# Attention and two gated layers on one core: the second layer's periods dealt in another order

## The chip, the cores and the metric

The kernel runs on one core of a Trainium2 chip. The metric is the device time of one execution in microseconds (us). TensorE (PE in the profile) does the matmuls, VectorE (DVE) and ScalarE (ACT) the work on their results, GpSimd (POOL) some sums and the DMAs that add into memory, SyncE (SP) issues the other DMAs.

## What is computed

A channel attention makes x (6016 tokens by 256), a first gated layer (silu) follows, and a second one (sigmoid), each with 1536 hidden units:

```python
def _moe2_ref(x, w_gate, w_val, w_out):
    gate = 1.0 / (1.0 + np.exp(-(x @ w_gate)))
    val = x @ w_val
    return (gate * val @ w_out).astype(np.float32)
```

## The kernel before

Every product of two fp32 matrices is made of three passes (`mm3`, lines 106 to 109): each operand is split into a rounded high part (a cast on ScalarE) and a low part (a subtraction on VectorE), and high·high, high·low and low·high are summed in PSUM. So a "product" below is three matmuls with 128 rows and 512 columns (448 in one of the six pairs of token blocks), and a "split" is a cast `hh` (line 618) and a subtraction `hl` (line 626).

The tokens are worked in six pairs of blocks, the hidden units in 12 blocks of 128. One step, a pair and a block of hidden units, is a **period**. The second layer has 72 of them, numbered here n = 0 to 71; the first twelve belong to the first pair, and so on. A period computes gate and value of two token blocks with seven products instead of eight (Strassen's scheme in Winograd's form), named after the operand: B11, T1, T4, T2, B21, T3, B22. T4 belongs to the period before. Four banks of PSUM hold them:

- Z ("g"): B11, then T2 added, then T3 added. After B11 ScalarE copies it to A, after T2 it copies it out as `g1`, after T3 two engines read it: ScalarE copies it to D (line 792), VectorE adds `e5` to it, which gives `v1` (line 798). Two engines never read one bank at once: the second waits for the first. B11 of the next period overwrites Z.
- B ("g"): T1, copied to `e5`; then B22 is added, and VectorE adds it to `g1` (line 804).
- A ("v"): B21 is added, ScalarE makes the gate `sg0` of it (line 785).
- D ("v"): T4 is added a period later, VectorE multiplies it by the gate (`fourth`, lines 551 and 553).

The sigmoid of `g1` (line 733) and the other gated product follow early in the next period. The gated values (`hs`) of six periods make a **team**, whose product with `w_out` is again Strassen's: seven kinds of operand, three blocks each, so 21 **output products**. They are done in the six periods that follow, three or four in each, between the seven others (`out`, `out_product`). Each needs its operand split first (`split_high`, `split_low`); `split_high(ahead)` goes at most so many splits ahead of the products. `hidden` lends the buffers of split values, three each for `hh` and `hl`. Results of output products are gathered in `r` (`gather`, called by `flush`): for the first team of a pair mostly by copies on ScalarE, for the second by additions on VectorE. `third_sum` and `first_sum` add gated values; some additions go as accumulating DMAs from POOL's queue (`more`, line 571).

Nothing reorders the work: each engine runs its instructions in the order in which the program's lines issue them (`manual_schedule`). In each period, hooks (`at("early")`, `at("ACT")`, `at("DVE")`, `at("end")`) also run the splits of the next pair's seven input operands (`pair_high` at periods 3 to 9 of every twelve, `pair_low` at 4 to 10, lines 366 and 369) and the sums that three or four of these need, as additions on POOL (`pair_sums`, `pair_sum`, line 398). "Position" below is n modulo 12; at positions 0 and 6 a team starts.

Of the kernel before, what the change touches and what calls it, by code (L numbers as in the profile page):

```python
# [10 lines left out]
F32 = mybir.dt.float32  # L11
# [6 lines left out]
P = 128  # L18
# [7 lines left out]
def kernel(  # L26
# [411 lines left out]
    def hidden(name):  # L438
        return ip3.tile([P, 512], F32R, tag=name, name=name)
# [171 lines left out]
    def split_high(ahead):  # L611
        while job and job["split"] < min(LAST, job["done"] + ahead):
# [77 lines left out]
    def period(it, pv, n, outs=()):  # L690


        s = {}
        slot = slots.popleft() if slots else {}
        outs = deque(partial(out_mm, *o, c) for o in outs for c in range(KC))
        n1 = n - len(stream0)
# [5 lines left out]
        def fourth(s):  # L702
            l, p, f = s["it"]
            w = hw[p]
            product(s["v0"], s["it"], T4, A22, False)
            gated(s["h"][:, 0, :w] if l else s["v0"], s["v0"], s["sg0"], l and f % 2)

        def split(ahead):
            if n1 >= 0:
                split_high(ahead)  # L710
                split_low()

        def out(count):
            for _ in range(count):
                if outs:
                    outs.popleft()()
                elif n1 >= 0:
                    out_product()

        if it:  # L720
            l, p, f = it
            w = hw[p]
            s["it"] = it
            act = (AF.Silu, AF.Sigmoid)[l]
# [5 lines left out]
        if pv:  # L730
            pl, pp, pf = pv["it"]
            pw = hw[pp]
            nc.scalar.activation(out=pv["g1"], in_=pv["g1"], func=(AF.Silu, AF.Sigmoid)[pl])  # L733
            gated(pv["v1"], pv["v1"], pv["g1"], pl and pf % 2 == 0)
        flush()
        if n1 > 0 and n1 % HALF == 0:
            team_start(n1 // HALF - 1)
        if n1 > 0 and pf % 2:
            third_sum(n1 - 1)
        split(2)  # L740
        if not it:
            while job["done"] < LAST:
                split(3)
                out_product()
                flush()
            return
        nc.scalar.copy(A, Z)  # L747
        if pv and pl == 0:
            hh1, hl1 = hidden("hh"), hidden("hl")
            nc.scalar.copy(hh1[:, :pw], pv["v1"])  # L750
            nc.vector.tensor_sub(hl1[:, :pw], pv["v1"], f32(hh1[:, :pw]))  # L751
            hid[pl, pp, 1, pf] = hh1, hl1
            fourth(pv)
        e5 = sp.tile([P, 512], F32, tag="e5", name="e5")[:, :w]
        if pv and pl:
            nc.scalar.copy(e5, B)
            if n1 > 0:
                split_high(3)
            fourth(pv)
            gw_load(n1 + 2)  # L760
            split_low()
            if pf % 2 == 0:
                first_sum(n1 - 1)
        at("early")
        if not (pv and pl):
            nc.scalar.copy(e5, B)
        else:
            out(1 if n1 % 2 == 0 else 0)
# [4 lines left out]
        if pv and pl == 0:  # L773
            hh0, hl0 = hidden("hh"), hidden("hl")
            nc.scalar.copy(hh0[:, :pw], pv["v0"])
            nc.vector.tensor_sub(hl0[:, :pw], pv["v0"], f32(hh0[:, :pw]))
            hid[pl, pp, 0, pf] = hh0, hl0
        flush()
        if n1 % 2 == 0:
            split(3)  # L780
        if n1 >= 0:
            out(2 if outs else 1)
            at("DVE")
        s["sg0"] = ip2.tile([P, 512], F32, tag="sg", name="sg")[:, :w]
        nc.scalar.activation(out=s["sg0"], in_=A, func=act)  # L785
        if n1 < 0:
            out(2)
            at("ACT")
            at("DVE")
        product(Z, it, T3, S3, False)  # L790
        D = s["v0"] = gv_bank("v")[:, :w]
        nc.scalar.copy(D, Z)  # L792
        if l:
            s["h"] = h_tile()
            s["v1"] = s["h"][:, 1, :w]
        else:
# [352 lines left out]
```

## Time and profile before

| | |
|---|---|
| median of 3 runs | 1227.27 us (1225.7 to 1228.14) |
| the profiled execution, its own time | 1227.86 us |
| its span, first to last instruction | 1225.8 us |
| TensorE busy | 96% of the span |
| VectorE, ScalarE busy | 74%, 69% |
| second layer's periods 1 to 71 | from 684 to 1202 us |
| the last team's products, after the last period | 1202 to 1226 us |

A matmul's end is modelled in the profile, so that busy time of TensorE hides gaps; the gap is seen in the start times, which are 0.227 us apart for 512 columns when nothing waits. The granted clock of TensorE is full in the second layer.

### The profile page before, as it was taken

To read this page: it belongs to the slowest core of one execution; us is meant where nothing else is said; L and a number is where in the kernel's file an instruction comes from. 1 tells how busy PE (TensorE), PEld (TensorE's weight loads), DVE (VectorE), ACT (ScalarE), POOL (GpSimd) and SP (SyncE) were. 2 spreads that over 40 slices of the span, in tenths; PEclk is the share of its full clock that TensorE was granted. 3 is DMA by queue.
4 is the path that set the end of the run, shared out by engine and by line. 5 is a ranking of instruction groups with operands and counts; after the bars stand their busy time and mean duration, and the time that the engine had idled before them with its cause. 6 is when DMAs were issued, how large, how long until landed. Compare 5 with 4: busy or idle time off the path is not lost.

```text
span 1225.8 us, 15986 instructions
## 1 busy us (share of the span) xinstructions
PE 1178.7 (96%) x5290; PEld 966.1 (79%) x5290; DVE 911.7 (74%) x1382; ACT 847.5 (69%) x1591; POOL 281.1 (23%) x327
## 2 busy tenths in 40 slices
PE   8898999999999999999999999999999999999997
PEld 7787777788899788888888677777777777778895
DVE  6798888876566566666665577887887888887877
ACT  6665667765566676677666677677777777777775
POOL 0043655553200200200200111311311311311121
PEclk9899999999999999999999999999999999999999
DMA  9662434766301301201430578988988988988995
GB/s 334 245 221 87 131 107 158 260 224 207 111 1 28 97 26 35 95 26 35 155 99 1 168 200 248 263 247 244 267 251 239 275 246 239 277 239 248 271 251 140
DMA packets 100946, 214.43 MB, mean 175 GB/s; under 512 B 10240, under 2 KB 35840, under 8 KB 100864
## 3 DMA queue, kind: packets, MB, share of 16 engines
q1 hardware_dynamic: 86896, 188.65, 46.2%
q0 software_dynamic: 13824, 24.65, 11.1%
q8 instruction: 41, 0.67, 0.2%
q14 instruction: 41, 0.34, 0.1%
q10 hardware_dynamic: 144, 0.13, 0.0%
HBM read 150.87 MB, written 37.88 MB: 154 GB/s over the span
## 4 chain that ended last, share of the span: by engine, by line
PE 62%; DVE 11%; ACT 4%; issue 4%; DMA 1%; POOL 0%; SPq 0%; DVEq 0%; ACTq 0%; POOLq 0%
PE g L107 10%; PE g L108 9%; PE g L109 9%; PE v L107 4%; PE v L108 4%; PE y L108 4%; PE v L109 4%; PE y L109 4%; PE y L107 4%; PE at L108 3%; PE at L109 3%; PE at L107 3%; DVE hl L626 2%; DVE g L804 2%; ACT v L792 1%
## 5 line engine op out<-in xcount | busy, mean ns | idle before, releaser
L571 POOL DMA_DIRECT2D hs<-hs x96 | 83.6, 914 | 466.1 <-DVE hl L626 197.3
L626 DVE TENSOR_TENSOR hl<-hs,hh 128x512 fp32r<-128x512 f32 (+1 forms) x216 | 152.5, 714 | 20.5 <-ACT hh L618 19.7
L733 ACT ACTIVATE g<-g 128x512 f32<-128x512 f32 (+1 forms) x120 | 74.7, 623 | 121.9 <-DVE g L804 121.9
L618 ACT CAST hh<-hs 128x512 fp32r<-128x512 f32 (+1 forms) x216 | 130.1, 609 | 4.6 <-PE y L109 1.4
L792 ACT COPY v<-g 128x512 f32<-128x512 f32 (+1 forms) x120 | 67.2, 560 | 65.8 <-PE g L109 65.1
L772 ACT COPY g<-g 128x512 f32<-128x512 f32 (+1 forms) x120 | 69.4, 578 | 44.7 <-PE g L109 44.0
L798 DVE TENSOR_TENSOR hs<-g,e 128x512 f32<-128x512 f32 (+1 forms) x72 | 48.9, 680 | 50.1 <-ACT v L792 50.1
L804 DVE TENSOR_TENSOR g<-g,g 128x512 f32<-128x512 f32 (+1 forms) x120 | 79.7, 664 | 0.0
L107 PE MATMUL g<-xh,gw 128*128 128x512 f32 x180 | 73.0, 405 | 5.7 <-DVE hs L798 4.9
L785 ACT ACTIVATE sg<-v 128x512 f32<-128x512 f32 (+1 forms) x120 | 71.1, 592 | 3.7
L107 PE MATMUL g<-qh,wh 128*128 128x512 f32 x168 | 66.8, 397 | 6.6 <-ACT wh L187 5.3
L798 DVE TENSOR_TENSOR v<-g,e 128x512 f32<-128x512 f32 (+1 forms) x48 | 32.4, 675 | 53.9 <-ACT v L792 53.9
L747 ACT COPY v<-g 128x512 f32<-128x512 f32 (+1 forms) x120 | 68.0, 567 | 4.8 <-PE g L109 0.3
L108 PE MATMUL g<-xl,gw 128*128 128x512 f32 x180 | 70.3, 391 | 0.0
L109 PE MATMUL g<-xh,gw 128*128 128x512 f32 x180 | 70.2, 390 | 0.0
L109 PE MATMUL g<-qh,wl 128*128 128x512 f32 x168 | 66.3, 395 | 1.9 <-DVE wl L196 1.9
L108 PE MATMUL g<-ql,wh 128*128 128x512 f32 x168 | 66.0, 393 | 0.0
L108 PE MATMUL y<-hl,ow 128*128 128x512 f32 (+1 forms) x144 | 57.2, 397 | 9.1 <-DVE hl L626 9.0
L451 ACT CAST hh<-v 128x512 fp32r<-128x512 f32 x48 | 28.1, 585 | 48.5 <-DVE v L449 48.5
L107 PE MATMUL v<-qh,wh 128*128 128x512 f32 x144 | 57.9, 402 | 3.3 <-DVE hl L457 3.3
L751 DVE TENSOR_TENSOR hl<-v,hh 128x512 fp32r<-128x512 f32 (+1 forms) x48 | 32.7, 681 | 32.4 <-ACT hh L750 32.4
L109 PE MATMUL v<-qh,wl 128*128 128x512 f32 x144 | 56.6, 393 | 0.0
(230 smaller groups left out, 3650.2 us busy)
## 6 DMA issues: line engine op xcount, KB each, us to landing
gw<-gd SPq DMA_DIRECT2D x144, 448.0 KB, 5.5
ow<-od SPq DMA_DIRECT2D x84, 384.0 KB, 5.1
hs<-hs POOLq DMA_DIRECT2D x80, 256.0 KB, 6.7
wraw<-in_w_dram SPq DMA_DIRECT2D x24, 768.0 KB, 5.4
vraw<-in_v_t_dram SPq DMA_DIRECT2D x11, 512.0 KB, 3.8
gd<-w2h SPq DMA_DIRECT2D x12, 448.0 KB, 2.6
gd<-w2l SPq DMA_DIRECT2D x12, 448.0 KB, 3.5
yd<-yo SPq DMA_DIRECT2D x20, 256.0 KB, 2.9
```

The costliest lines, as they stand in the source:

```text
L107: nc.tensor.matmul(ps, sh, mh, start=start, stop=False, skip_group_check=more)
L108: nc.tensor.matmul(ps, sh, ml, start=False, stop=False, skip_group_check=more)
L109: nc.tensor.matmul(ps, sl, mh, start=False, stop=stop, skip_group_check=more)
L571: nc.gpsimd.dma_start(out=to, in_=t, accum_op=ALU.add)
L618: nc.scalar.copy(h, src)
L626: nc.vector.tensor_sub(lo, src, f32(h))
L733: nc.scalar.activation(out=pv["g1"], in_=pv["g1"], func=(AF.Silu, AF.Sigmoid)[pl])
L772: nc.scalar.copy(s["g1"], Z)
L785: nc.scalar.activation(out=s["sg0"], in_=A, func=act)
L792: nc.scalar.copy(D, Z)
L798: nc.vector.tensor_add(s["v1"], Z, e5)
L804: nc.vector.tensor_add(s["g1"], s["g1"], B)
```

## The change

`period` is divided into two functions: `period` for the first layer, where the order of the instructions stays, and `team_period` for the second layer. In the second layer:

- `hidden` lends four buffers each for `hh` and `hl` (for the whole kernel), and `split_high` may be four ahead of the output products; its argument is now the most splits that one call makes.
- After T3, VectorE adds `v1` first, and ScalarE copies Z to D second.
- The copies of Z to A and of B to `e5` come before any split of the period; two splits follow, whose `hl` stand behind `fourth`; one more `hh` and `hl` stands behind the copy to `g1`, one behind the gate, two more at the end where a buffer is free.
- No output product stands between T4 and T2. There is one after B21, and at the period's end three in even and two in odd periods (before: one more after T4 in even periods, two at the end).
- `third_sum` stands ahead of the gathering.

```diff
     def hidden(name):
-        return ip3.tile([P, 512], F32R, tag=name, name=name)
+        return ip3.tile([P, 512], F32R, tag=name, name=name, bufs=4)
...
-    def split_high(ahead):
-        while job and job["split"] < min(LAST, job["done"] + ahead):
+    def split_high(most):
+        while job and most and job["split"] < min(LAST, job["done"] + 4):
+            most -= 1
...
+    def team_period(it, pv, n, outs):
...
+        if n and pf % 2:
+            third_sum(n - 1)
         flush()
...
         nc.scalar.copy(A, Z)
...
+        nc.scalar.copy(e5, B)
+        split_high(2)
+        fourth(pv)
+        split_low()
...
         product(Z, it, T2, S2, False)
         product(A, it, B21, A12, False)
...
+        split(1)
+        out(2 if outs else 1)
...
+        nc.scalar.activation(out=s["sg0"], in_=A, func=AF.Sigmoid)
+        at("DVE")
         flush()
+        split(1)
         product(Z, it, T3, S3, False)
         D = s["v0"] = gv_bank("v")[:, :w]
+        s["h"] = h_tile()
+        s["v1"] = s["h"][:, 1, :w]
+        nc.vector.tensor_add(s["v1"], Z, e5)
         nc.scalar.copy(D, Z)
+        at("ACT")
         product(B, it, B22, S4, False)
         nc.vector.tensor_add(s["g1"], s["g1"], B)
+        split(2)
...
-            out(max(2, len(outs)))
+            out(max(3 - n % 2, len(outs)))
```

VectorE's order in period 33 (position 9) before, from its addition to `g1` at the end of period 32 to its own `v1` (L626 is `hl`, L551 the product with the second gate, L553 `fourth`, L559 `first_sum`, L369 a split of the next pair's input, L798 `v1`):

```order
L804 TENSOR_TENSOR g_8825<-g_8825,g 128x512
L626 TENSOR_TENSOR hl<-hs,hh 128x512
L551 SCALAR_TENSOR_TENSOR hs<-hs,g_8825 128x512
L626 TENSOR_TENSOR hl<-hs,hh 128x512
L553 TENSOR_TENSOR hs<-v,sg 128x512
L626 TENSOR_TENSOR hl<-hs,hh 128x512
L559 TENSOR_TENSOR t<-hs 128x512
L369 TENSOR_TENSOR ql<-xs,qh 128x512
L798 TENSOR_TENSOR hs<-g,e_8879 128x512
```

and now (L627 is `hl`, L831 `v1`):

```order
L835 TENSOR_TENSOR g_8827<-g_8827,g 128x512
L551 SCALAR_TENSOR_TENSOR hs<-hs,g_8827 128x512
L553 TENSOR_TENSOR hs<-v,sg 128x512
L627 TENSOR_TENSOR hl<-hs,hh 128x512 x2
L559 TENSOR_TENSOR t<-hs 128x512
L627 TENSOR_TENSOR hl<-hs,hh 128x512
L369 TENSOR_TENSOR ql<-xs,qh 128x512
L627 TENSOR_TENSOR hl<-hs,hh 128x512
L831 TENSOR_TENSOR hs<-g,e_8875 128x512
```

Between `fourth` and `v1` stand six instructions now, three before; ahead of `fourth` stand fewer.

ScalarE's order at the end of the same period and the start of the next, with the engines that each instruction waits for, before (L785 is the gate, L792 the copy to D, L668 a gathering, L618 `hh`, L733 the sigmoid of `g1`):

```order
L785 ACTIVATE sg<-v 128x512 [waits PE_49]
L792 COPY v<-g 128x512 [waits DVE_49,PE_49]
L668 COPY r<-y 128x512
L618 CAST hh<-hs 128x512 [waits Activation_49]
L366 CAST qh<-ql 128x512
L733 ACTIVATE g_8901<-g_8901 128x512 [waits DVE_49]
```

and now (L832 is the copy to D, L788 the sigmoid, L801 the copy to A):

```order
L669 COPY r<-y 128x512 [waits PE_49]
L619 CAST hh<-hs 128x512 [waits DMASW5_49,Activation_49]
L832 COPY v<-g 128x512 [waits DVE_49]
L366 CAST qh<-ql 128x512
L788 ACTIVATE g_8901<-g_8901 128x512 [waits DVE_49]
L801 COPY v<-g 128x512 [waits PE_49,Activation_49]
```

The copy to D waits for VectorE, whose `v1` waits for TensorE; a split and the gathering moved ahead of it.

TensorE's order where a team starts (period 30, position 6), from T4 (`v`) to the team's first output product (`y`), before:

```order
L107 MATMUL v<-xh,gw 128x512
L108 MATMUL v<-xl,gw 128x512
L109 MATMUL v<-xh,gw 128x512
L107 MATMUL y<-hh,ow 128x512
L108 MATMUL y<-hl,ow 128x512
L109 MATMUL y<-hh,ow 128x512
```

and now:

```order
L107 MATMUL v<-xh,gw 128x512
L108 MATMUL v<-xl,gw 128x512
L109 MATMUL v<-xh,gw 128x512
L107 MATMUL g<-xh,gw 128x512
L108 MATMUL g<-xl,gw 128x512
L109 MATMUL g<-xh,gw 128x512
L107 MATMUL v<-xh,gw 128x512
L108 MATMUL v<-xl,gw 128x512
L109 MATMUL v<-xh,gw 128x512
L107 MATMUL y<-hh,ow 128x512
L108 MATMUL y<-hl,ow 128x512
L109 MATMUL y<-hh,ow 128x512
```

The first output product stands two products later in its period.

## Rows read from the trace of the kernel before

**Rows 1.** Page, part 1: busy us (share of the span) and instructions by engine

```profile
PE 1178.7 (96%) x5290; PEld 966.1 (79%) x5290; DVE 911.7 (74%) x1382; ACT 847.5 (69%) x1591; POOL 281.1 (23%) x327
```

**Rows 2.** Windows by stage: us, busy time (instructions) by engine, clock, DMA share, GB/s

```profile
684.15:714.38 30.23, 26.77 (x105) 18.86 (x105) 17.70 (x26) 19.31 (x35) 7.08 (x6) 1.00 0.79 239
714.38:1120.26 405.88, 395.40 (x1701) 316.28 (x1700) 337.65 (x516) 304.06 (x566) 85.88 (x88) 1.00 0.87 250
```

**Rows 3.** Waits of TensorE's weight loads, 684 to 1202 us: total us, times, longest

```profile
PEld y L108 <- DVE hl L626: 11.7, 11, 1.3
PEld g L107 <- DVE hs L798: 10.6, 9, 1.4
PEld g L107 <- ACT v L747: 7.6, 17, 0.5
```

**Rows 4.** Timeline, ScalarE: the same sigmoid in periods 24 and 36 (start, duration, what)

```profile
857.36 0.63 ACT L733 ACTIVATE g<-g 128x512 f32<-128x512 f32 x1 [0.81 <-DVE g L804]
...
947.88 0.64 ACT L733 ACTIVATE g<-g 128x512 f32<-128x512 f32 x1 [0.81 <-DVE g L804]
```

**Rows 5.** Timeline, TensorE, period 33: first of B11, last of T4, last of T3, next B11

```profile
918.16 0.39 PE L107 MATMUL g<-xh,gw 128*128 128x512 f32 x1
...
919.97 0.39 PE L109 MATMUL v<-xh,gw 128*128 128x512 f32 x1
...
922.69 0.39 PE L109 MATMUL g<-xh,gw 128*128 128x512 f32 x1
...
924.96 0.39 PE L107 MATMUL g<-xh,gw 128*128 128x512 f32 x1
```

**Rows 6.** Timeline, VectorE, period 33: `fourth` and what follows, to `v1`

```profile
920.40 0.69 DVE L553 TENSOR_TENSOR hs<-v,sg 128x512 f32<-128x512 f32 x1 [0.20 <-PE v L109]
921.01 0.68 DVE L626 TENSOR_TENSOR hl<-hs,hh 128x512 fp32r<-128x512 f32 x1
...
922.21 0.68 DVE L369 TENSOR_TENSOR ql<-xs,qh 128x512 fp32r<-128x512 f32 x1
923.72 0.69 DVE L798 TENSOR_TENSOR hs<-g,e 128x512 f32<-128x512 f32 x1 [0.83 <-ACT v L792]
```

**Rows 7.** Timeline, ScalarE, period 33: the copy to D, and a cast behind it

```profile
923.12 0.57 ACT L792 COPY v<-g 128x512 f32<-128x512 f32 x1 [0.76 <-PE g L109]
...
924.60 0.63 ACT L366 CAST qh<-ql 128x512 fp32r<-128x512 f32 x1
```

**Rows 8.** Timeline, TensorE, period 30: a team's first output product waits for its `hl`

```profile
896.88 0.39 PE L107 MATMUL y<-hh,ow 128*128 128x512 f32 x1
898.13 0.50 PE L108 MATMUL y<-hl,ow 128*128 128x512 f32 x1 [0.86 <-DVE hl L626]
898.47 0.40 PE L109 MATMUL y<-hh,ow 128*128 128x512 f32 x1
```

**Rows 9.** Timeline, period 27 (position 3): VectorE and POOL, and the B11 behind it

```profile
873.51 2.34 DVE L626 TENSOR_TENSOR hl<-hs,hh 128x512 fp32r<-128x512 f32 x1
875.77 0.68 DVE L553 TENSOR_TENSOR hs<-v,sg 128x512 f32<-128x512 f32 x1
...
879.18 0.68 DVE L798 TENSOR_TENSOR hs<-g,e 128x512 f32<-128x512 f32 x1
...
873.66 1.63 POOL L398 TENSOR_TENSOR xs<-zl,ql 128x512 f32<-128x512 f32 x1
...
879.91 0.50 PE L107 MATMUL g<-xh,gw 128*128 128x512 f32 x1 [0.93 <-DVE hs L798]
```

**Rows 10.** Timeline, POOL, period 28 (position 4): the sum for T4 of the next pair

```profile
886.83 1.29 POOL L398 TENSOR_TENSOR xs<-ql,xs 128x512 f32<-128x512 f32 x1 [3.22 <-ACT v L792]
```

**Rows 11.** Timeline, TensorE, period 2, without output products: B11 waits for `v1`

```profile
689.55 0.50 PE L107 MATMUL g<-xh,gw 128*128 128x512 f32 x1 [0.69 <-DVE hs L798]
```

**Rows 12.** Timeline, VectorE, after the last period: splits 11 to 13, the last split, the last gathering

```profile
1213.30 1.70 DVE L626 TENSOR_TENSOR hl<-hs,hh 128x448 fp32r<-128x448 f32 x3
...
1220.97 0.61 DVE L626 TENSOR_TENSOR hl<-hs,hh 128x448 fp32r<-128x448 f32 x1
1222.34 0.62 DVE L680 TENSOR_TENSOR r<-r,at 128x448 f32<-128x448 f32 x1 [0.76 <-PE at L109]
```

More of the change, by code (lines that the diff above doesn't have):

```diff
@@ L700, in at @@
                 fn()
[L702 to L711, printed above, removed]
+        l, p, f = it
+        w = hw[p]
+        Z = gv_bank("g")[:, :w]
+        product(Z, it, B11, A11, True)
+        A = gv_bank("v")[:, :w]
+        B = gv_bank("g")[:, :w]
+        product(B, it, T1, S1, True)
+        if pv:
+            nc.scalar.activation(out=pv["g1"], in_=pv["g1"], func=AF.Silu)
+            nc.vector.tensor_mul(pv["v1"], pv["v1"], pv["g1"])
+        nc.scalar.copy(A, Z)
+        if pv:
+            parts(pv, 1, pv["v1"])
+            fourth(pv)
+        at("early")
+        e5 = sp.tile([P, 512], F32, tag="e5", name="e5")[:, :w]
+        nc.scalar.copy(e5, B)
+        product(Z, it, T2, S2, False)
+        product(A, it, B21, A12, False)
+        s["g1"] = sp2.tile([P, 512], F32, tag="g1", name="g1")[:, :w]
+        nc.scalar.copy(s["g1"], Z)
+        if pv:
+            parts(pv, 0, pv["v0"])
+        s["sg0"] = ip2.tile([P, 512], F32, tag="sg", name="sg")[:, :w]
+        nc.scalar.activation(out=s["sg0"], in_=A, func=AF.Silu)
+        for _ in range(2):
+            outs.popleft()()
+        at("ACT")
+        at("DVE")
+        product(Z, it, T3, S3, False)
+        D = s["v0"] = gv_bank("v")[:, :w]
+        nc.scalar.copy(D, Z)
+        s["v1"] = sp.tile([P, 512], F32, tag="t0", name="v1")[:, :w]
+        nc.vector.tensor_add(s["v1"], Z, e5)
+        product(B, it, B22, S4, False)
+        nc.vector.tensor_add(s["g1"], s["g1"], B)
+        while outs:
+            outs.popleft()()
+        at("end")
+        return s
+    def team_period(it, pv, n, outs):
+        s = {"it": it}
+        slot = slots.popleft() if slots else {}
+        outs = deque(partial(out_mm, *o, c) for o in outs for c in range(KC))
+        def at(point):
+            for fn in slot.get(point, ()):
+                fn()
         def out(count):
@@ L716, in out, with split @@
                     outs.popleft()()
-                elif n1 >= 0:
+                else:
                     out_product()
+        def split(most):
+            split_high(most)
+            split_low()
         if it:
```

102 lines of the change are left out of this document (39 added, 63 removed).

## The prediction, made before the changed kernel ran

> **What bounds the kernel now.** The page's first part [rows 1] says TensorE, busy 96% of the span, ahead of VectorE with 74%. The windows by stage come next [rows 2]: the change touches the second layer alone, so 684 us to the end, and the steady part of it, from the first team at 714 us, is where its new order acts. How much TensorE loses there is read from start times. One product takes 0.68 us (T4's last matmul ends the third product: 919.97 + 0.23 - 918.16 = 2.04) [rows 5]. Twelve periods hold 12 x 7 + 2 x 21 = 126 products, 85.7 us; the same sigmoid twelve periods apart is 90.5 us apart [rows 4]. So 4.8 us in twelve periods are waits, of which I can put 4.55 to places; the rest is spread over the starts and stays. The waits of the weight loads name them [rows 3]: a team's first output product waits for its `hl`, 11 times; B11 waits for `v1`, 9 times; T2 or another product of Z waits for a copy on ScalarE, 17 times. I made the list by position in the twelve: 1.14 us at position 6 [rows 8], 0.67 at 0, the same wait; 2.1 at positions 3 and 4, where POOL holds VectorE up [rows 9]; 0.32 each at 7 and 11, T2 behind the copy to A.
>
> **What the change takes away.** At a team's start the first output product stands two products (1.36 us) later, and its split stands behind fewer things: 1.14 and 0.67 go at a start where VectorE is in time. The copy to A stands ahead of splits and directly behind the sigmoid, so the two 0.32 go. The wait at position 3 is VectorE's lateness, to be worked out anew. No instruction is added or removed on any engine; SP's and POOL's DMAs keep their order, only their place in the period shifts by less than one period, and the landing that matters (accumulated `hs`, used some two periods on, 14 us) stays far off. In periods 1 to 5, which have no output products, B11 waits for both readers of Z in turn [rows 11]; 0.69 then 0.57 us is as long as 0.57 then 0.69, so nothing changes there. The first layer keeps its order; a fourth buffer there has no wait to remove.
>
> **What it adds: the copy to D now waits for VectorE, and B11 for the copy.** Take the quiet period 33, clock zero at B11's first matmul (918.16). T4's result can be read at 2.24, where `fourth` began; VectorE's instructions follow each other by 0.60 ((922.21 - 920.40) / 3) [rows 6]. T3's result can be read at 4.96, when the copy to D began [rows 7]. Before, VectorE had three instructions between `fourth` and `v1` and was free at 4.65; it sat idle 0.83 us until the copy was done [rows 6]. B11 is due at 6.80 after ten products (odd periods) [rows 5], at 7.48 after eleven (even). From the start of `v1` Z comes free after 0.69 + 0.03 + 0.57 + 0.06 = 1.35 us: its own duration, the copy's [rows 6, 7], and two handovers (923.12 + 0.57 to 923.72; 879.18 + 0.68 to 879.91) [rows 7, 9].
>
> With k instructions between `fourth` and `v1`, `v1` starts at 2.24 + 0.605 (k + 1), and Z is free 1.35 later: k = 3 at 6.3 (T3 decides), 4 at 6.6, 5 at 7.2, 6 at 7.8. Counted in the new order, k by position 0 to 11 is 4, 5, 3, 6, 5, 4, 5, 6, 4, 6, 5, 3 (before 2 to 4 everywhere). Even periods have 7.48 and are in time with all of them. Odd ones are not: k = 5 costs 0.43 (position 1), k = 6 costs 1.03 (positions 3, 7, 9). Each stall also costs 0.11 for the matmul that resumes (898.13 to 898.47 is 0.34 against 0.23) [rows 8]. First order: 0.43 + 3 x 1.03 + 4 x 0.11 = 4.0 us in twelve periods, against 4.55 taken away. By this alone the change would be worth nothing, and the second order decides.
>
> **Second order.** Each is a delay on an engine that no longer has slack.
> - Position 3: three sums on POOL, 1.63 us each. A VectorE instruction with both operands in SBUF waits until such a sum ends (873.66 + 1.63 = 875.29, the `hl` ends 0.56 later, having taken 2.34 us); one that reads PSUM does not (875.77, 0.68 us) [rows 9]. In the new order POOL comes to these sums at the end of position 2, from about 0.8 us before to 4.3 us after B11, and the first `hl` behind `fourth` (2.85) waits for the third: +1.3. Bounds: 0, were the sums over in time, and 3.2, were three instructions blocked as in period 27 (the first by 2.34 - 0.69 = 1.65, the two others together by about as much). I take 1.3, since POOL runs as soon as its queue lets it.
> - Position 4: the sum for the next T4, 1.29 us [rows 10], starts when the cast's low part is done (4.75) and holds one `hl` up: `v1` at 6.6, Z at 7.95, +0.45 and 0.11. Below: 0.
> - Position 5: the copy to D ends as B11 starts, a cast of the next pair stands behind it (0.52 from one start to the next, 924.60 to the next sigmoid) [rows 7], so the sigmoid starts at 0.36, and two gatherings stand ahead of `fourth`: +0.42 and 0.11. Below: 0.15.
> - Position 6: the same lateness, then `third_sum` and a gathering; the team's first `hl` ends at 4.1 and is wanted at 3.63: 0.56 and 0.22. So half of the team-start wait stays where the sixth period is full; at position 0 it goes.
> - Position 7: two casts behind the late copy, then a gathering before the copy to A; `hl` waits for `hh`: +0.37.
>
> Together 1.3 + 0.56 + 0.53 + 0.78 + 0.37 = 3.5, so 7.5 against 4.55: **+2.95 in twelve periods**, four times (periods 12 to 59) +11.8. Periods 6 to 11 have positions 6, 7, 9: 2.9 against 1.7, +1.2. Periods 60 to 71 have no next pair and 448 columns: by the same steps (product 0.595, VectorE 0.54 apart, (1.70 - 0.62) / 2 [rows 12]) 3.0 against 2.6, +0.4.
>
> **The end.** After the last period VectorE is the longest queue. The fourth buffer lets the last `hl` pass the two gatherings ahead of it: from split 11 (1213.30) twelve instructions of 0.54 to its start at 1219.8 (before 1220.97); then three gatherings, the last at 1221.4 (before 1222.34) [rows 12]. -0.9. Bounds 0 and -2.
>
> Sum: 1.2 + 11.8 + 0.4 - 0.9 = +12.5 on the profiled execution, 1227.86 (span 1225.8 and 2.1 around it); the median is 0.6 lower. 1227.27 + 12.5 is 1239.8; since two of the second-order terms have zero as lower bound and none of them leans down further, I say **1239**.
>
> **The rivals.**
> - *First order alone.* The sums on POOL fall between VectorE's instructions and the casts find room: 4 x (4.0 - 4.55) - 0.9 + 0.6 = -2.5, so 1224.8, at the edge of no change. For it: ScalarE has about a quarter idle. Against it: VectorE would have no gap between 2.24 and `v1` in odd periods, so any sum of POOL finds it busy with SBUF operands.
> - *Faster: the repeated gaps go and none comes.* If `v1` were not late, because `hl` found room elsewhere, the steady waits (22 us over the six pairs, 4.55 in each full twelve) and 0.9 at the end would go: 1204. It decides from k = 4 down in odd periods. For it: the removed waits are real [rows 3, 8]. Against it: six instructions of 0.60 between 2.24 and 4.96 do not fit. The Trainium skill has a rule that speaks for this rival: in Perfetto Trace Analysis, Optimization Strategy, it says that the same gap repeating on the engine that should be saturated can mean too few buffers for the next tile. By that rule the fourth buffer alone would close the gaps, and this would be the likely case. The trace does not agree where it can be read: the repeated gap at a team's start ends with VectorE's `hl` [rows 8], not with a buffer's return.
> - *Slower still.* All of POOL's 3.2 us at position 3 land on the path, and the lateness of one odd period reaches the even one behind it: +1.9 and some 0.5 in each twelve, four times, +10: 1249.
>
> **How the numbers follow.** Forecast (1231 to 1245 by its own bounds) 0.70; first order alone 0.13; faster 0.12; slower still 0.05. A measurement tells 0.2%, 2.5 us, from no change. Slower by that: 0.70 + 0.05, less some of the forecast's lower edge, plus nothing of the others: 0.73. First order alone lies on the border, most of it counted as the same: 0.09. Faster: 0.12 and a part of that border: 0.18. The range leaves out the faster rival and the slowest: 1222 to 1246.
>
> **What would show it.** After: `fourth` on VectorE waits for T4 and then runs without idle time to `v1` in odd periods; the copy to D on ScalarE waits for `v1`, and B11 for that copy, by about 1 us at positions 3, 7, 9 and 0.4 at 1; the team starts at position 0 without a wait, at 6 with half a us; the same sigmoid twelve periods apart is 93 us apart instead of 90.5; periods 1 to 5 stay at 30.2 us together [rows 2]. The forecast is wrong if even positions stall, or if VectorE is idle before `v1` in odd ones.

## The result, and the profile of the changed kernel

The changed kernel takes 1235.57 us (median of 7), the kernel before 1225.70 (median of 7, same chip, side by side): a ratio of 1.0081, 95% interval 1.0056 to 1.0105. It is slower, by 9.9 us. The profiled execution took 1238.83 us, with a span of 1237.0 us (before 1227.86 and 1225.8).

The engines do the same instructions as in [rows 1], the same number on each; TensorE's busy time is 3 us longer, and the rest of the 11.2 us is idle time. Part 1 of the page of the changed kernel:

```profile
PE 1181.7 (96%) x5290; PEld 966.6 (78%) x5290; DVE 904.9 (73%) x1382; ACT 845.5 (68%) x1591; POOL 278.0 (22%) x327
```

**By stage.** The windows view, cut at the second layer's sigmoids of periods 0, 6, 60 and 72, of the changed kernel (us from the start, length, busy time by engine with instructions, granted clock, DMA share, GB/s). In period 0 the line of the sigmoid still makes the first layer's last silu; its start is called the second layer's first sigmoid here.

```profile
677.50:715.80 38.30, 34.49 (x141) 25.30 (x140) 22.98 (x34) 26.00 (x45) 7.08 (x6) 1.00 0.62 189
715.80:1130.10 414.30, 396.32 (x1700) 315.25 (x1699) 329.40 (x516) 302.07 (x567) 84.28 (x88) 1.00 0.85 245
1130.10:1212.00 81.90, 79.88 (x380) 70.55 (x379) 63.47 (x108) 58.96 (x119) 13.93 (x16) 1.00 0.85 240
1212.00:1237.00 25.00, 18.23 (x68) 13.14 (x67) 17.72 (x32) 11.74 (x22) 5.24 (x6) 0.87 0.65 156
```

and of the kernel before, the same four stages (periods 0 to 5, 6 to 59, 60 to 71, and the end):

```profile
675.80:714.40 38.60, 35.04 (x142) 25.33 (x141) 22.27 (x34) 25.70 (x45) 7.08 (x6) 1.00 0.62 187
714.40:1120.30 405.90, 395.42 (x1701) 316.32 (x1700) 337.65 (x516) 304.08 (x566) 85.88 (x88) 1.00 0.87 250
1120.30:1201.90 81.60, 80.23 (x380) 70.40 (x379) 63.37 (x108) 58.68 (x118) 13.87 (x16) 1.00 0.86 241
1201.90:1225.80 23.90, 16.82 (x67) 11.23 (x65) 17.79 (x32) 11.98 (x22) 5.23 (x6) 0.96 0.65 162
```

Periods 6 to 59 are 8.4 us longer with the same 1700 matmuls; TensorE's busy time there is 0.9 us more, so 7.5 us are waits. Periods 0 to 5 are 0.3 shorter, 60 to 71 are 0.3 longer, the end 1.1. The remaining 1.7 us of the span's 11.2 lie in front of the second layer: its first sigmoid is at 677.5 us, against 675.8 before. That part varies by more than this over the profiled executions (last section), so they are compared here from that sigmoid on: 559.5 us against 550.0, +9.5.

**Which waits.** The view of waits of TensorE's weight loads, 684 to 1212 us, of the changed kernel (total us, times, longest), beside [rows 3]:

```profile
PEld g L107 <- ACT v L832: 36.9, 35, 1.9
PEld y L108 <- DVE hl L627: 4.8, 11, 0.8
...
PEld g L107 <- ACT v L801: 1.9, 5, 0.5
```

The team start's wait for `hl` (11.7 us before) is down to 4.8, and the wait for the copy to A (7.6 before) to 1.9. In their place stands one wait of 36.9 us: B11 (line 107, into `g`) for the copy to D (line 832, which was 792). Those totals count the weight load's own wait, which begins earlier than TensorE's loss; the loss is read from the starts.

**The quiet period.** Timeline of period 33 in the changed kernel (start, duration, instruction, idle time before it and who ended it), VectorE from `fourth` on, against [rows 6]:

```profile
926.43 0.69 DVE L553 TENSOR_TENSOR hs<-v,sg 128x512 f32<-128x512 f32 x1 [1.13 <-PE v L109]
927.03 1.29 DVE L627 TENSOR_TENSOR hl<-hs,hh 128x512 fp32r<-128x512 f32 x2
928.24 0.68 DVE L559 TENSOR_TENSOR t<-hs 128x512 f32<-128x512 f32 x1
928.84 0.69 DVE L627 TENSOR_TENSOR hl<-hs,hh 128x512 fp32r<-128x512 f32 x1
929.44 0.69 DVE L369 TENSOR_TENSOR ql<-xs,qh 128x512 fp32r<-128x512 f32 x1
930.04 0.68 DVE L627 TENSOR_TENSOR hl<-hs,hh 128x512 fp32r<-128x512 f32 x1
930.64 0.68 DVE L831 TENSOR_TENSOR hs<-g,e 128x512 f32<-128x512 f32 x1
```

then ScalarE's copy to D, against [rows 7]:

```profile
931.36 0.57 ACT L832 COPY v<-g 128x512 f32<-128x512 f32 x1 [1.49 <-DVE hs L831]
```

and TensorE, the last matmul of the period and B11, against [rows 5]:

```profile
930.76 0.39 PE L109 MATMUL at<-hh,ow 128*128 128x512 f32 x1
931.99 0.50 PE L107 MATMUL g<-xh,gw 128*128 128x512 f32 x1 [0.84 <-ACT v L832]
```

VectorE has six instructions between `fourth` and `v1` (line 831) and not a moment idle; `v1` starts at 930.64, where 926.43 + 0.605 x 7 = 930.67 puts it. The copy to D follows it, and B11 starts at 931.99, 1.35 us after `v1`, instead of at 930.76 + 0.23 = 930.99. The stall of 1.00 us is the one that the prediction worked out (1.03), instruction by instruction.

The same sigmoid in periods 24 and 36, ScalarE's timeline, against [rows 4]: twelve periods take 92.6 us instead of 90.5.

```profile
853.48 0.63 ACT L788 ACTIVATE g<-g 128x512 f32<-128x512 f32 x1 [0.18 <-DVE g L835]
...
946.05 0.63 ACT L788 ACTIVATE g<-g 128x512 f32<-128x512 f32 x1 [0.18 <-DVE g L835]
```

**Position 3** (period 27), VectorE, POOL and the B11 behind it, against [rows 9]:

```profile
876.27 1.15 DVE L551 SCALAR_TENSOR_TENSOR hs<-hs,g 128x512 f32<-128x512 f32 x1 [0.70 <-ACT g L788]
...
879.07 1.90 DVE L627 TENSOR_TENSOR hl<-hs,hh 128x512 fp32r<-128x512 f32 x2
...
878.53 1.29 POOL L398 TENSOR_TENSOR xs<-zl 128x512 f32<-128x512 f32 x1
...
884.64 0.50 PE L107 MATMUL g<-xh,gw 128*128 128x512 f32 x1 [1.45 <-ACT v L832]
```

Two `hl` in a row take 1.90 us beside POOL's third sum and 1.29 us in period 33: +0.61. B11's stall is 1.72 us with its restart (the 0.11 us by which the matmul behind a wait is late), against 1.11 in period 33.

### The profile page after: what moved, and what is told of

Read it like the earlier page. It is cut to its first block, busy times and chain, and to the rows that moved or that the text cites. A ratio compares the mean times of both kernels' runs of the same rounds, so it can differ in the third digit from the quotient of the medians.

```text
span 1237.0 us, 15879 instructions
## 1 busy us (share of the span) xinstructions
PE 1181.7 (96%) x5290; PEld 966.6 (78%) x5290; DVE 904.9 (73%) x1382; ACT 845.5 (68%) x1591; POOL 278.0 (22%) x327
## 3 DMA queue, kind: packets, MB, share of 16 engines
q0 software_dynamic: 13824, 24.65, 11.3%
## 4 chain that ended last, share of the span: by engine, by line
PE 51%; DVE 12%; issue 10%; ACT 5%; DMA 3%; POOL 1%; SPq 0%; DVEq 0%; POOLq 0%; ACTq 0%
PE g L107 8%; PE g L109 8%; PE g L108 8%; DVE hl L627 5%; PE v L107 4%; PE v L109 4%; PE v L108 4%; PE y L108 3%; PE y L109 3%; PE y L107 3%; PE at L108 3%; PE at L109 2%; PE at L107 2%; DVE hs L831 2%; POOL hs L571 1%
## 5 line engine op out<-in xcount | busy, mean ns | idle before, releaser
L627 DVE TENSOR_TENSOR hl<-hs,hh 128x512 fp32r<-128x512 f32 (+1 forms) x216 | 144.8, 698 | 9.7 <-ACT hh L619 8.9
L619 ACT CAST hh<-hs 128x512 fp32r<-128x512 f32 (+1 forms) x216 | 127.1, 617 | 7.6 <-DMA hs<-hs 2.2
L832 ACT COPY v<-g 128x512 f32<-128x512 f32 (+1 forms) x72 | 40.4, 561 | 115.2 <-DVE hs L831 115.2
L702 DVE TENSOR_TENSOR hl<-v,hh 128x512 fp32r<-128x512 f32 (+1 forms) x96 | 65.0, 678 | 61.0 <-ACT hh L701 60.7
L107 PE MATMUL g<-xh,gw 128*128 128x512 f32 x180 | 73.3, 407 | 12.5 <-ACT v L832 12.4
L724 ACT ACTIVATE g<-g 128x512 f32<-128x512 f32 (+1 forms) x47 | 29.1, 619 | 61.9 <-DVE g L751 61.9
L701 ACT CAST hh<-v 128x512 fp32r<-128x512 f32 (+1 forms) x96 | 56.7, 591 | 9.0 <-DVE v L725 4.1
L107 PEld LDWEIGHTS g<-xh,gw 128*128 128x128 f32 x180 | 33.7, 187 | 30.6 <-ACT v L832 20.5
L108 PE MATMUL v<-ql,wh 128*128 128x512 f32 x144 | 56.7, 393 | 0.0
L108 PE MATMUL at<-hl,wh 128*128 128x512 f32 (+1 forms) x144 | 56.0, 389 | 0.5 <-DVE hl L702 0.2
L107 PE MATMUL at<-hh,wh 128*128 128x512 f32 (+1 forms) x144 | 55.7, 387 | 0.6 <-DVE yo L481 0.6
```

The lines of the kernel that those rows point to most:

```text
L107: nc.tensor.matmul(ps, sh, mh, start=start, stop=False, skip_group_check=more)
L108: nc.tensor.matmul(ps, sh, ml, start=False, stop=False, skip_group_check=more)
L619: nc.scalar.copy(h, src)
L627: nc.vector.tensor_sub(lo, src, f32(h))
L701: nc.scalar.copy(hh[:, :w], v)
L702: nc.vector.tensor_sub(hl[:, :w], v, f32(hh[:, :w]))
```

## The experiments

The theory is that VectorE's in-order queue between `fourth` and `v1` decides. The change puts the copy to D behind `v1`, so that B11 waits for `v1` and one copy more, and it puts more instructions ahead of `v1`. First rival: the new dealing of output products or the splits cost the time, not the readers' order. Second rival: POOL's sums. "Positions" are periods counted in twelve, and stalls are what TensorE's starts are further apart than 0.23 us, averaged over periods 12 to 59.

### The readers' order, put back in the changed kernel

```diff
-        nc.vector.tensor_add(s["v1"], Z, e5)
         nc.scalar.copy(D, Z)
+        nc.vector.tensor_add(s["v1"], Z, e5)
```

> The changed kernel with one pair of lines exchanged: after T3 ScalarE copies Z to D first, VectorE adds v1 second, as before the change. Theory (VectorE's queue between fourth and v1, and the copy to D behind v1): Z is free 0.75 us after the start of v1 instead of 1.35, so the stalls of odd periods fall from 1.0 to 0.4 us (positions 7 and 9), from 0.4 to 0 (position 1), from 1.6 to 1.0 (position 3), and those of positions 4 to 6 shrink, since the casts no longer stand behind a late copy: some 3.5 us less in twelve periods, 17 us in all, about 7 us faster than the kernel before. Rival (the later output products or the fourth buffer cost the time, the order of the two readers does not matter): as the changed kernel, 10 us slower than before.

1220.85 us, 0.9947 [0.9928, 0.9967]: this one line makes the changed kernel faster than the kernel before, and is worth 1.3%. Period 33 in this run, VectorE's `v1` (now line 832), then TensorE:

```profile
917.32 0.69 DVE L553 TENSOR_TENSOR hs<-v,sg 128x512 f32<-128x512 f32 x1 [1.48 <-PE v L109]
...
921.54 0.69 DVE L832 TENSOR_TENSOR hs<-g,e 128x512 f32<-128x512 f32 x1
...
922.28 0.50 PE L107 MATMUL g<-xh,gw 128*128 128x512 f32 x1 [0.24 <-DVE hs L832]
```

`v1` is just as late behind `fourth` as in the changed kernel (4.22 us here, 4.21 there), but the copy to D is done by then, and B11 follows `v1` directly: a stall of 0.51 in place of 1.11. Twelve periods take 89.2 us, with 3.1 us of stalls (changed kernel 6.2, before 4.4).

### The readers' order alone, in the kernel before

```diff
-        nc.scalar.copy(D, Z)
         if l:
             s["h"] = h_tile()
             s["v1"] = s["h"][:, 1, :w]
+            nc.vector.tensor_add(s["v1"], Z, e5)
+            nc.scalar.copy(D, Z)
...
```

> The kernel before with only the readers of Z exchanged in the second layer: VectorE first, ScalarE second. Theory: VectorE has two to four instructions between fourth and v1 there and is in time, so Z comes free when it did; only position 3, where POOL's sums make v1 late, loses 0.6 us, four times, and the five periods without output products 0.08 each: 3 us slower than before. Rival (the order of the readers costs by itself): about 10 us slower than before.

1231.67 us, 1.0036 [1.0016, 1.0055]. Where VectorE has fewer instructions ahead of `v1`, the same swap costs 0.36% and not 1.3%. So what the swap costs depends on what else the change does; that the longer queue makes it dear fits the runs below. The size is near the 3 us that were expected, the place is not: position 3 loses 0.1 us (1.61 against 1.51), positions 5, 7 and 9 lose 0.4 to 0.8, in part in waits of T2 for the copy to A (line 747), and positions 0 and 4 gain 0.5 each. Waits of TensorE's weight loads, 715 to 1205 us; line 796 is the copy to D, a wait that the kernel before does not have:

```profile
PEld g L107 <- ACT v L747: 13.7, 21, 1.1
PEld g L107 <- ACT v L796: 10.3, 9, 1.9
```

### One VectorE instruction fewer ahead of `v1`

The low part of the split behind the gate goes behind the copy to D; `v1` stays first.

```diff
-        split(1)
+        split_high(1)
...
         nc.scalar.copy(D, Z)
+        split_low()
```

> The changed kernel with the low part of the split that follows the gate moved behind v1, so that one instruction less stands between fourth and v1 in periods that have it; VectorE still reads Z first. Theory: v1 starts 0.6 us earlier, the stalls fall by 0.6 at positions 3, 7 and 9 and to nothing at 1 and 4: some 2.9 us less in twelve periods, 14 us in all, 4 us faster than the kernel before. Rival (k is not what makes v1 late): as the changed kernel.

1219.16 us, 0.9925 [0.9907, 0.9942]: faster than the kernel before, and by about twice what was expected. Stalls at positions 7 and 9 are 0.49 each where the changed kernel has 1.34 and 1.09; k = 5 (k is the number of VectorE's instructions between `fourth` and `v1`) gives 0.54 by the prediction's rule. The stall at position 1 vanished; at position 3 it did not move (1.60), although 0.6 less was expected. The reason stands in POOL's queue. Its accumulating DMA there waits for the `hl` that was moved, and the three sums stand behind that DMA. Period 27 in this run, POOL, then VectorE:

```profile
864.52 0.86 POOL L571 DMA_DIRECT2D hs<-hs  x1 [0.97 <-DVE hl L627]
865.08 1.62 POOL L398 TENSOR_TENSOR xs<-zl,ql 128x512 f32<-128x512 f32 x1
...
868.38 1.83 POOL L398 TENSOR_TENSOR xs<-zl 128x512 f32<-128x512 f32 x1
...
868.38 2.38 DVE L627 TENSOR_TENSOR hl<-hs,hh 128x512 fp32r<-128x512 f32 x2
```

The third sum ends 4.76 us after B11 (865.45) instead of 3.59, and the two `hl` take 2.38 us instead of 1.90: 1.09 lost against 1.29, where the changed kernel loses 0.61. What the shorter queue gained, the later sums took.

### The dealing of output products alone, in the kernel before

```diff
-        else:
-            out(1 if n1 % 2 == 0 else 0)
...
-            out(max(2, len(outs)))
+            out(max(2 if n1 < 0 else 3 - n1 % 2, len(outs)))
```

> The kernel before with only the output products dealt as in the change: none between T4 and T2, three at the end of even periods. Theory: the waits at the team starts (1.14 us at position 6, 0.67 at 0) go, but T2 now follows T4 in even periods too and waits some 0.3 us for the copy to A at positions 0, 6 and 8, where casts or a gathering stand ahead of it: 1 us less in twelve periods, 3 to 5 us faster than before in all. Rival (the later products are what costs): slower than before by several us.

1244.55 us, 1.0134 [1.0116, 1.0152], the wrong side of what was expected. Waits of TensorE's weight loads, 730 to 1100 us:

```profile
PEld y L108 <- DVE hl L626: 16.6, 16, 1.3
...
PEld at L108 <- DVE hl L626: 6.1, 8, 0.8
```

Three output products in a row at the end of a period want three splits in time, and at the old places of the splits they come late: 22.7 us of waits for `hl`. So the later dealing needs earlier splits, as the change brings along; with them and with the old readers' order the first run gains 0.5%. The splits alone, without the new dealing, were not run.

### Both repairs at once, and three other places for the low part

The first two repairs of the changed kernel together: the copy to D first, then `v1`, then the low part.

```diff
-        split(1)
+        split_high(1)
...
+        nc.scalar.copy(D, Z)
         nc.vector.tensor_add(s["v1"], Z, e5)
-        nc.scalar.copy(D, Z)
+        split_low()
```

> The changed kernel with both edits at once: ScalarE's copy to D first and VectorE's v1 second, and the low part of the split that follows the gate behind v1. Theory: with one instruction less in VectorE's queue and Z free 0.75 us after the start of v1, odd periods are in time (k = 5: 5.87 + 0.75 = 6.6 against 6.8); what stays in twelve periods is 0.4 at position 3 (POOL's sums), 0.7 at position 6 (a team's first split) and some jitter, 87.3 us instead of 89.2 and 89.6 with one edit alone: 10 us faster than either, 1211 us, 1.2 to 1.3% faster than before. Rival (both edits remove the same wait): as either alone, 0.6% faster.

1233.15 us, 1.0067 [1.0042, 1.0093]: 22 us more than expected. Period 33, VectorE, then TensorE with T1's first matmul:

```profile
926.48 0.69 DVE L832 TENSOR_TENSOR hs<-g,e 128x512 f32<-128x512 f32 x1 [0.27 <-ACT v L831]
927.09 0.68 DVE L627 TENSOR_TENSOR hl<-hs,hh 128x512 fp32r<-128x512 f32 x1
927.69 0.68 DVE L836 TENSOR_TENSOR g<-g,g 128x512 f32<-128x512 f32 x1
...
928.42 0.50 PE L107 MATMUL g<-xh,gw 128*128 128x512 f32 x1 [0.23 <-DVE g L836]
```

`v1` now waits for the copy to D, the low part stands behind it, and only then comes g1's add, which frees the other shared bank, B. T1, which writes the bank next, waits for that add, 12.5 us in 22 waits from 715 to 1205 us; so does the next sigmoid. There are two deadlines, not one. T1 is not all of the loss, though. Periods 12 to 59 are 11.3 us longer than with the copy first alone (367.4 against 356.1): T1's stalls and the starts behind them make some 5.6, three falls of TensorE's clock some 4.6 (last section), and position 3 some 3.2, where POOL's sums end 5.6 us after B11 and not 3.6; positions 7 and 9 gain 2.4.

The next run was set up together with this one, to see whether a still shorter queue ahead of `v1` gains anything. It puts one instruction more between `v1` and g1's add, and so bears on T1 as well.

```diff
-        at("DVE")
...
         split_low()
+        at("DVE")
```

> As e5_both, and also the low part of the next pair's input split behind v1, one more instruction less between fourth and v1 at positions 4 to 10. Theory: odd periods are already in time in e5_both, so nothing is left to gain there: the same time within 2 us; position 4 may gain 0.1. Rival (VectorE's queue still sets the period): faster by another 0.6 at positions 7 and 9, 5 us.

1242.33 us, 1.0152 [1.0127, 1.0177]: slower again by 9 us, where no change was expected, with T1 stalled by about 1.0 behind positions 7 and 9, though no instruction was added and `v1` has one fewer ahead. And the other way, on the run before it: the low part behind g1's add.

```diff
-        split_low()
...
         nc.vector.tensor_add(s["g1"], s["g1"], B)
+        split_low()
         split(2)
```

> The changed kernel with the D copy ahead of v1's add and with the low part of the split after the gate moved behind g1's add (in the run that put it between v1 and g1's add, T1 and the next sigmoid came late). If that explanation holds, v1 is late by nothing but the D copy, nothing stands ahead of g1's add, and both earlier gains are there: under 89.0 us from a sigmoid to the one twelve periods on, T1's stalls of 0.3 to 0.4 us gone, and about 1211 us, at a ratio of 0.986 to 0.992 to the kernel before. If instead any third instruction between the gate and the next period's products costs the same wherever it stands, this gives the 1.0067 of that run again, within 0.004.

1224.57 us, 0.9991 [0.9967, 1.0014]. T1's waits are gone and the time fell by 0.76%, so for T1 the place was the cause and not the mere number; but it stayed some 13 us above the 1211 expected. At position 3 TensorE still waits 1.5 to 1.8 us: POOL's sums, later again, end 5.75 us after B11 there, and two `hl` take 3.45 us together. And the low part is now late for its own reader. Period 30, TensorE:

```profile
897.53 0.39 PE L107 MATMUL at<-hh,ow 128*128 128x512 f32 x1
898.23 0.50 PE L108 MATMUL at<-hl,ow 128*128 128x512 f32 x1 [0.31 <-DVE hl L627]
```

Such waits for `hl` and the starts behind them make some 0.7 us at position 0 and 1.1 at position 6. The same place with `v1` first, as in the change:

> The changed kernel with v1 first, as it is, and the low part of the split after the gate behind g1's add rather than behind v1 (that run: 0.9925). If what stands between v1 and g1's add costs time here too, this is faster than that run by 1 to 4 us, 0.989 to 0.992. If v1 first leaves g1's add enough time, it gives the same as that run within 0.002.

1222.29 us, 0.9967 [0.9946, 0.9987], the other side of what was expected: behind g1's add is 0.4% worse than behind `v1`. Here the low part's own reader is not the reason, since the waits for `hl` make 2.0 us in periods 12 to 59 in both runs. Of the 3.0 us by which these periods are longer (360.7 against 357.7), 1.5 are position 3, where POOL's DMA waits for the moved `hl` and the sums end 5.07 us after B11 instead of 4.76, and 1.4 are one fall of the clock behind the longest stall there (2.24 us). So the low part has no place without a price: between a late `v1` and g1's add T1 waits for it, and behind g1's add POOL's sums do.

### POOL's sums

```diff
-        t = ip3.tile([P, 512], F32, tag="yo", name="xs")[:, :w]
-        nc.gpsimd.tensor_sub(t, *ab)
-        sums[out] = t
+        sums[out] = ab[0]
```

> The changed kernel without POOL's four sums for each next pair (the splits of T1 to T4 take another operand instead, so the second layer's results are others; all else runs as it did). Theory: VectorE isn't held up at positions 3 and 4; the stall at 3 falls from 1.6 to 1.0, that at 4 from 0.6 to 0, and 5 and 6 a little: 1.5 us less in twelve periods, 6 us in all, still 0.3% slower than before. Rival (POOL does not matter, the stall at 3 is the queue's length alone): 0.8% slower, as the changed kernel.

1227.92 us, 1.0025 [1.0005, 1.0045]. Position 3 falls from 1.61 to 1.10, which is the count of six instructions alone (1.14), position 4 from 0.63 to none, position 5 from 0.32 to 0.16; positions 7 and 9 stay (1.36, 1.09). So POOL's part is 0.5 at position 3 and 1.3 of the 6.2 us of stalls in twelve periods; 4.9 stay without it. Of the net slowdown it is more than half, since from the second layer's first sigmoid on the 9.5 us fall to 4.3 (554.3 us against 550.0). But the kernel before has the same sums, and it was not run without them, so this is no share of what the change did.

Then the sums were kept, but on VectorE, behind g1's add, one in each of four periods (on top of the run with the low part behind `v1`):

```diff
-        nc.gpsimd.tensor_sub(t, *ab)
+        (eng or nc.gpsimd).tensor_sub(t, *ab)
...
+        pair_sum(l, p, out, a, b, nc.vector)
...
-                    slots[2].setdefault("end", []).append(partial(pair_sums, *nxt))
...
+                        for i, x in enumerate(((T1, T3, B11), (T3, B22, T3), (T2, B22, T1), (T4, B21, T2))):
+                            slots[1 + i].setdefault("end", []).append(partial(vector_sum, *nxt, *x))
...
```

> The run with the low part behind v1 (0.9925) with, in the second layer, the next token pair's four sums on VectorE instead of POOL, one behind g1's add in each of four periods. Of that run's 1.60 us of stall at position 3, what the sums cost by slowing VectorE goes: if POOL's sums are what is left there beside the VectorE instructions ahead of v1 (0.49 at positions 7 and 9 with the same number of them), position 3 falls to 0.5 and twelve periods to about 88.5 us, 1213 to 1216 us in all, a ratio of 0.988 to 0.991. If the sums only cost elsewhere what they cost here (four more instructions of 0.6 us on VectorE, which is the engine that TensorE waits for), the ratio stays at 0.9925 within 0.002.

1217.31 us, 0.9923 [0.9896, 0.9950]. The times do not tell it from the run without it, as the second of the two expectations had it. The trace does, and it follows the first: position 3 went from 1.60 to 0.50, periods 12 to 59 from 357.7 to 352.9 us, and from the layer's first sigmoid to the end it is 539.8 us against 544.3. Its profiled execution came to that sigmoid 3.9 us later (675.8 against 671.9), in work that the edit does not touch. What the times alone would show of this step is open; that the stall went is shown.

### The last instruction ahead of `v1`

On top of that, the low part of the token pair's split (line 369 in the timeline above) goes behind g1's add:

```diff
-        at("DVE")
...
         split(2)
+        at("DVE")
```

> The run before this one (sums on VectorE) with the low part of the token pair's split, which stands between the gate and T3's product in periods 4 to 10 of each twelve, moved to the end of the period, behind g1's add. One VectorE instruction fewer ahead of v1 at positions 7 and 9, where 0.49 us of stall each is left: by the count rule (0.6 us for each instruction ahead of v1 as long as v1 is late) both go, 1.0 us per twelve periods, 5 us in all, a ratio of 0.984 to 0.987. If the instruction makes the next gated value late instead (it then stands right ahead of it), the gain is lost, and the ratio is that of the run before this one or up to 0.004 above.

**1207.85 us, 0.9855 [0.9828, 0.9883]**: the fastest of all, 1.45% below the kernel before and 2.2% below the changed kernel. Period 33, VectorE, ScalarE's copy to D, and TensorE around B11:

```profile
907.33 0.69 DVE L559 TENSOR_TENSOR hs<-v,sg 128x512 f32<-128x512 f32 x1 [1.48 <-PE v L109]
...
910.35 0.69 DVE L836 TENSOR_TENSOR hs<-g,e 128x512 f32<-128x512 f32 x1
...
911.07 0.57 ACT L837 COPY v<-g 128x512 f32<-128x512 f32 x1 [0.29 <-DVE hs L836]
...
911.67 0.40 PE L109 MATMUL at<-hh,ow 128*128 128x512 f32 x1
911.90 0.40 PE L107 MATMUL g<-xh,gw 128*128 128x512 f32 x1
```

Four instructions ahead of `v1`: the bank is free at 910.35 + 1.35 = 911.70, B11 is due at 911.90 and starts there. The readers' order is the change's, VectorE first, and it costs nothing in this period. Twelve periods take 86.9 us, of which 0.9 are stalls; the largest left is position 3, where five instructions still stand ahead of `v1` (0.50).

### The fourth buffer

```diff
-        return ip3.tile([P, 512], F32R, tag=name, name=name, bufs=4)
+        return ip3.tile([P, 512], F32R, tag=name, name=name, bufs=3)
...
-        while job and most and job["split"] < min(LAST, job["done"] + 4):
+        while job and most and job["split"] < min(LAST, job["done"] + 3):
```

> The changed kernel with three buffers for split values instead of four, and splits at most three ahead of the products. Theory (the fourth buffer neither causes nor covers much, since VectorE's queue has the same length): 0.8% slower than before, as the changed kernel, give or take 3 us. Rival (with products dealt three in a row the splits need the fourth buffer, as the late hl of e4_before_outs_late suggest): TensorE waits for hl at the products, 0.3 to 1 us in most periods, and the kernel is 1.3% slower than before or worse.

1236.56 us, 1.0106 [1.0074, 1.0138]: the interval holds the changed kernel's 1.0081 and the rival's 1.013, so the times do not decide. The trace does: twelve periods take 93.0 us against 92.6, with 6.5 us of stalls against 6.2. The fourth buffer does remove waits for `hl` (15.8 us in the weight loads' waits from 715 to 1205 us with three, 4.8 with four), but the waits for the copy to D are longer with four (32.2 against 26.8 with three), and 0.4 us in twelve periods is what is left of it; position 7 stalls 1.08 with three and 1.34 with four, position 5 0.90 and 0.32, positions 1, 3 and 9 the same within 0.03. The Trainium skill (Perfetto Trace Analysis, Optimization Strategy) has the hint that a repeating gap can mean too few buffers. In the changed kernel it does not lead to the cause of the repeated gap of 1.1 us; the fourth buffer alone in the kernel before was not run.

## Why the prediction was right, and where its terms were off

The forecast was 1239 us with a range of 1222 to 1246, and slower at 0.73; measured were 1235.57, 9.9 us above the kernel before at its side. The reason was right too: the copy to D behind `v1`, and VectorE's count ahead of it. That the sum came so near is in part luck, since periods 12 to 59 were taken 4.2 us too dear and the end 2.0 us too cheap. Point by point, by the prediction's own sum:

| term, us | predicted | in the trace |
|---|---|---|
| position 1 (with restart) | 0.54 | 0.51 |
| position 3: count 1.14, POOL 1.3 | 2.44 | 1.61 (1.72 in all but the last) |
| position 4 | 0.56 | 0.63 |
| position 5 | 0.53 | 0.32 |
| position 6 | 0.78 | 0.64 |
| position 7 | 1.51 | 1.34 |
| position 9 | 1.14 | 1.09 |
| all, in twelve periods | 7.5 | 6.2 |
| taken away | 4.55 | 4.4 |
| periods 12 to 59 | +11.8 | +7.6 |
| periods 6 to 11, and 60 to 71 | +1.6 | +1.1 |
| periods 0 to 5 | 0 | -0.3 |
| the end | -0.9 | +1.1 |
| sum | +12.5 | +9.5 |

- **First order: right.** The three counts of six and the count of five are met within 0.1 us where nothing else acts (positions 1 and 9; position 3 without POOL's sums 1.10 against 1.14). The run with one instruction less gave 0.49 where the rule says 0.54, the one with two less gave none.
- **The term that was mis-sized: POOL at position 3.** 1.3 was taken, 0.6 came. The prediction let the third sum end 4.3 us after B11; it ended at 879.82, 3.6 us after (B11's first matmul is at 876.23): the sums began 1.0 us ahead of B11 and not 0.8, and the third took 1.29 us and not 1.63. So two `hl` lost 0.61 us together. This one step is 0.7 to 0.8 of the 1.3 us by which the twelve periods were overestimated. The Trainium skill (SBUF — State Buffer, Who interferes with whom) has a VectorE instruction with two SBUF inputs contend with a POOL instruction that reads SBUF, and calls the contention on their shared ports an exclusive lock. The trace agrees, in that a VectorE instruction of 0.69 us takes 1.15 in the changed kernel (876.27) and 2.34 in the one before [rows 9]; how much of it lands on the path was the question, and it was put too high.
- **The step that failed: the end.** A gain of 0.9 was forecast and 1.1 us were lost. The sum took VectorE's queue for what decides there; the landing of the accumulated `hs`, which come by DMA from POOL's queue, it had put down as far off. The fourth buffer did what was said of it: the last `hl` passes the two gatherings and stands directly behind its cast. But that cast waits for the last accumulating DMA, now and before, and in 11 of the 14 profiled executions here; this is read from the traces, no run tested it. POOL's DMA and the cast, in the changed kernel with the `hl` behind it, then before (its `hl` is at 1220.97 [rows 12]):

```profile
1224.77 0.86 POOL L571 DMA_DIRECT2D hs<-hs  x1 [0.21 <-issue]
1231.37 0.57 ACT L619 CAST hh<-hs 128x448 fp32r<-128x448 f32 x1 [0.95 <-DMA hs<-hs]
1231.97 0.62 DVE L627 TENSOR_TENSOR hl<-hs,hh 128x448 fp32r<-128x448 f32 x1 [0.90 <-ACT hh L619]
```

```profile
1214.22 0.86 POOL L571 DMA_DIRECT2D hs<-hs  x1 [0.29 <-DVE hl L626]
1219.86 0.57 ACT L618 CAST hh<-hs 128x448 fp32r<-128x448 f32 x1 [0.54 <-DMA hs<-hs]
```

  Counted from the last sigmoid (1211.95, before 1201.92), the DMA is issued at 12.82 us (before 12.30) and the cast starts at 19.42 (before 17.94): 1.48 later, against the 0.5 us that the `hl` gains. Of the 1.48, 0.52 come with the later issue, and nearly as much is there from the beginning of the end, where T4's last matmul starts 0.70 us behind the sigmoid (before 0.29) and `fourth` 1.17 (before 0.70). The other 0.96 lie between issue and cast, 6.60 us against 5.64; why that took longer is open.

- **The rivals.** First order alone (1224.8) fell: the second-order terms are there, some 2.3 of the 6.2 us. The faster rival, in which `v1` is not late, was not this kernel, but its condition was right: it was to decide from k = 4 down, and with k = 4 at positions 7 and 9, and POOL's sums on VectorE, the fastest experiment has these gaps closed, at 1208 us (the rival said 1204). Of the 3.2 us of POOL's that the slower rival put on the path, 0.6 came.
- **What the prediction did not see.** It took the swap's cost and the longer queue's as one. The experiments part them: the dealing and splits with the old readers' order gain 0.5%, the swap costs 0.36% on the short queue and 1.3% on the long one. And it named one deadline behind VectorE's queue, Z. The runs with the low part moved show three more within an instruction or two of it: g1's add for T1, `hl` for the next output product, and `hl` for POOL's accumulating DMA, behind which the sums stand. Its last sign, that it is wrong if even positions stall, is at odds with its own sum, which has 0.56 at position 4 and 0.78 at 6; the trace has 0.63 and 0.64 there. Periods 1 to 5, which were to stay at 30.2 us from sigmoid to sigmoid, took 30.8, while from B11 to B11 they are 0.1 shorter (30.5 against 30.6).

## What to carry to other kernels

Where two engines read a shared bank in turn, count what stands in the first reader's queue between its last event from outside and that read, times its pace, plus the second read, and compare with the time at which the bank is wanted; here that sum was right to 0.1 us, and each instruction moved out was worth its 0.6 us until the gap was closed, at the positions where POOL's sums do not act. Count the same for every deadline behind the same queue before moving an instruction, those of other engines' queues too: in four of the six runs here that moved one, it, or what waits for it, stood in the way of something else. The order of the readers that cost 0.36% on a short queue cost 1.3% on a longer one, so the two are to be judged together.

## What the hardware showed that was not expected

**TensorE's clock after stalls.** In the run with the copy to D first and the low part behind g1's add, position 3 stalls by 1.84 us in periods 15, 27 and 39. Windows of 4 us behind the first two of these stalls (the columns as above):

```profile
784.20:788.50 4.30, 4.30 (x13) 3.35 (x13) 2.77 (x5) 2.74 (x5) 0.88 (x1) 0.60 0.30 73
876.00:880.00 4.00, 4.00 (x18) 3.25 (x18) 3.44 (x7) 3.66 (x7) 0.88 (x1) 1.00 0.36 89
```

Behind the first the granted clock is 0.60 for 4.3 us, with matmuls 0.43 us apart, most of it at the lower of the two levels (1.2 GHz); behind the second, which is as long, it stays at 1.00. The drop costs 1.6 us, nearly as much as the stall itself. With both repairs at once it came behind the stalls of 1.45 to 1.8 us at position 3 in three periods. In the changed kernel's end it came behind the wait of 2.02 us, with 0.51 from 1216.6 to 1220.1 us and matmuls of 448 columns 0.37 us apart; the kernel before waits 1.54 us at that place and has no such stretch there. Timeline of the changed kernel, TensorE:

```profile
1215.53 0.47 PE L108 MATMUL y<-hl,ow 128*128 128x448 f32 x1 [2.02 <-DVE hl L627]
...
1216.64 0.57 PE L107 MATMUL y<-hh,ow 128*128 128x448 f32 x1
1217.01 0.58 PE L108 MATMUL y<-hl,ow 128*128 128x448 f32 x1
```

In the end of the fastest run it was 0.55 from 1192.7 to 1195.9 us, behind a stretch of short waits (1188.4 to 1192.7 us), none of which put two matmuls' starts more than 1.0 us apart. What decides between two stalls of the same length was not found.

**The first layer's time.** The second layer's first sigmoid came between 670.4 and 678.6 us in the fourteen profiled executions, one of each kernel here, though all edits but the fourth buffer lie behind it. Between the runs with the sums on POOL and on VectorE the difference arises in the first 200 us. So two profiled executions can differ by up to 8 us before the second layer begins, and their stages are better compared from a common mark. How well a stage repeats from one execution to the next is not shown, since each kernel was profiled once.
